# Chunked attention in front of a mixture of experts: Q, K and V laid out by numpy before the launch, K's windows copied by GpSimd, row sums taken by VectorE

## The chip, the cores and the metric

One core of one Trainium2 chip runs the whole program. The metric is the device time of one execution in microseconds (us). The kernel before took 1106.13 us (median of three runs, 1105.65 to 1109.15). Engines are named PE (TensorE), DVE (VectorE), ACT (ScalarE), POOL (GpSimd) and SP (SyncE, which here only issues DMAs).

## The reference

```python
def _attn_ref(q, k, v, mem_k, mem_v):            # B,H,S,D = 4,8,768,64; 8 memory rows per head
    chunk, left_ctx, right_ctx = (32, 16, 8)
    for c in range(S // chunk):                   # 24 chunks of 32 query rows
        k_ctx = k[:, :, max(0, 32*c - 16):min(S, 32*c + 32 + 8)]      # v_ctx likewise
        k_full = np.concatenate([mem_k, k_ctx], axis=2)               # up to 8 + 56 rows
        scores = scale * np.matmul(q_c, k_full.transpose(0, 1, 3, 2))
        a = np.exp(scores - np.max(scores, axis=-1, keepdims=True))
        a = a / (np.sum(a, axis=-1, keepdims=True) + 1e-09)
        out[:, :, c_start:c_end] = np.matmul(a, v_full)
def reference(...):
    x = attn_out.transpose(0, 2, 1, 3).reshape(3072, 512)
    x = _moe_ref(x, ...)       # logits = xn @ en.T / tau; top 1 of 8 experts; relu(x @ w1[e]) @ w2[e] * gate
    return _moe2_ref(x, ...)   # r = relu(x @ w_in); (r * r) @ w_out
```

All data are float32; the output has shape [3072, 512].

## The kernel before

The program has three stages: attention (about the first 170 us), the expert layer with its routing (to about 560 us) and the dense layer (to the end). In the second and third stage each float32 operand is split into a high and a low fp32r part and each product is three matmuls.

**The attention loop.** Work is cut into 32 items: batch b, a pair of heads hp (two heads side by side fill 128 partitions or 128 columns), and a half of the sequence (384 rows, 12 chunks). A pair j is two items. A software pipeline runs 39 rounds; in round i the list `order` (L564 to L568) calls each stage for item i minus the lag written beside it, so stages of different items interleave in a fixed order on every engine. The engines take their own instructions strictly in that order.

- `load_qk`, `load_v` (L264, L289): SP issues the DMAs of a pair: Q and K in rows of 1 KB (four sequence rows of 64 floats), V by chunks in rows of 256 bytes, and the 8 memory rows of V, broadcast to every chunk.
- `relayout` (L321): POOL (`q2`) and ACT (`k2`) bring the two heads side by side.
- `stage_a` (L330): PE transposes Q and K (4 + 4 transposes); ACT copies Q^T from PSUM (`qt`) and K^T into the zero-padded block tile `kw` as 12 overlapping windows of 56 columns (two copies); POOL adds the 8 memory columns.
- `stage_b` (L353): 12 score matmuls, then DVE masks a few columns. `max_b`, `sub_b` on DVE, `exp_b` on ACT.
- `shift_v` (L387): two DVE copies fill rows 32 to 55 of each V window from the next chunk (for the last two pairs by DMA).
- `stage_c` (L397): three transposes of the exponentials, copied by ACT (`pt`). `stage_d` (L406): 12 matmuls with V; V has a column of ones per head, so column 64 is the row sum. `sum_d`, `inv_d`, `scale_d` on DVE divide.
- `stage_t` (L448): three transposes of the result, copied by DVE and ACT in turn (`xt`); after the last pair of a batch the rows go to the DRAM tile `x_d` (768 KB, issued by ACT). `stage_m` (L461): router logits with 32 stationary columns (the expert embeddings) and the 128 tokens streamed; `stage_u` transposes them back to `dots`.
- `square` (L442): sums of squares per token on ACT.

From item 24 on, `early` picks the busiest expert of the first three batches and starts its weight loads and its first matmuls between the stages (the dictionary at L1367 says in which rounds). After the loop the rest of the routing, the expert slots and the dense layer follow in a written order (the string at L1386 and the loop at L1444).

PSUM has eight banks: in the loop `ps_s`, `ps_t`, `ps_o` one each, `ps_a` three, `ps_l` two. In the dense layer, `compare` (L1227) transposes one block a second time as plain float32 and adds the flag "differs" (a zero) to the last output tile.

Of the kernel before, what the change touches and what calls it, by code (L numbers as in the profile page):

```python
# [9 lines left out]
F32 = mybir.dt.float32  # L10
# [11 lines left out]
def kernel(  # L22
# [6 lines left out]
    mem_v: bass.AP,  # L29
# [10 lines left out]
    B, H, S, D = q.shape  # L40
    NM = mem_k.shape[2]
# [5 lines left out]
    HP = H // 2  # L47
# [31 lines left out]
    big = ctx.enter_context(tc.tile_pool(name="big", bufs=1))  # L79
# [8 lines left out]
    win_h = big.tile([P, KD, F2], F32R, name="win_h")  # L88
    win_l = big.tile([P, KD, F2], F32R, name="win_l")
# [128 lines left out]
    def weight(kind, i, w1_e, w2_e):  # L218
# [3 lines left out]
        else:  # L222
# [7 lines left out]
            lambda kk=kk, c=slice(o * 512, (o + 1) * 512): (win_h[:, kk, c], win_l[:, kk, c]),  # L230
# [4 lines left out]
    def attention(actx, hooks, space, drain):  # L235
# [3 lines left out]
        v_ctx, kw_ctx, qn_ctx = (actx.enter_context(ExitStack()) for _ in range(3))  # L239
        vb_p = v_ctx.enter_context(tc.tile_pool(name="vb", bufs=1))  # L240
        kw_p = kw_ctx.enter_context(tc.tile_pool(name="kw", bufs=1))
        kn_p = qn_ctx.enter_context(tc.tile_pool(name="kn", bufs=1))
        qn_p = qn_ctx.enter_context(tc.tile_pool(name="qn", bufs=3))
        ps_a = actx.enter_context(tc.tile_pool(name="ps_a", bufs=3, space=PSUM))
        ps_s, ps_t, ps_o = ps_r
        ps_l = actx.enter_context(tc.tile_pool(name="ps_l", bufs=2, space=PSUM))

        NV, NW, NK_, LAG = 3, 3, 2, 4
        kn = [kn_p.tile([KP, 4, R * D], F32, name=f"kn{i}") for i in range(NK_)]
        kw = [kw_p.tile([P, NC, 2, 64], F32, name=f"kw{i}") for i in range(NW)]  # L250
        vb = [vb_p.tile([P, 2 * NC + 1, 2, D + 1], F32, name=f"vb{i}") for i in range(NV)]
        scratch = per.tile([P, TE * P // 2], F32, name="scratch")
        mkn = scratch[0:H * NM, 0:B * 2 * D].rearrange("p (b j d) -> p b j d", b=B, j=2)
        mkT = per.tile([P, HP, B, 2, NM], F32, name="mkT")
        en = scratch[0:E, B * 2 * D:B * 2 * D + DM]
        enT = per.tile([P, KD, 32], F32, name="enT")
# [3 lines left out]
        qn_t, x_t, st, qk2, lp = {}, {}, {}, {}, {}  # L260

        kf, vf = (z.rearrange("b h s d -> (b h s) d") for z in (k, v))

        def load_qk(j):  # L264
            b, hp, _ = ks[2 * j]
            h0 = 2 * hp
            t = qn_p.tile([QP, 2, 2, R, D], F32, name="qn", tag="qn", bufs=2)
            for half in range(2):
                qn_t[2 * j + half] = t[:, :, half]
            nc.sync.dma_start(  # L270
                out=t.rearrange("p h j r d -> p (h j) (r d)"),
                in_=q[b, h0:h0 + 2].rearrange("h (j p r) d -> p (h j) (r d)", j=2, r=R),
            )

            base = (b * H + h0) * S
            for g0, g1, p0, p1 in (
                [(0, 1, LEFT // R, KP), (1, 4, 0, KP)] if base == 0 else
                [(0, 3, 0, KP), (3, 4, 0, KP - RIGHT // R)] if base + 2 * S == B * H * S else
                [(0, 4, 0, KP)]
            ):  # L280
                nc.sync.dma_start(
                    out=kn[j % NK_][p0:p1, g0:g1],
                    in_=bass.AP(
                        tensor=k.tensor, offset=k.offset + (base + g0 * HALF + p0 * R - LEFT) * D,
                        ap=[[R * D, p1 - p0], [HALF * D, g1 - g0], [1, R * D]],
                    ),
                )

        def load_v(j):  # L289
            b, hp, _ = ks[2 * j]  # L290
            t = vb[j % NV]
            for hh in range(2):
                h = 2 * hp + hh
                p0 = 64 * hh
                base = (b * H + h) * S
                c0, c1 = int(base == 0), 2 * NC + int(base + S < B * H * S)
                if c0:
                    nc.sync.dma_start(out=t[p0 + LEFT:p0 + CH, 0, hh, 0:D], in_=v[b, h, 0:LEFT, :])
                nc.sync.dma_start(
                    out=t[p0:p0 + CH, c0:c1, hh, 0:D],  # L300
                    in_=vf[base + CH * c0 - LEFT:base + CH * c1 - LEFT].rearrange("(c p) d -> p c d", p=CH),
                )
                if c1 == 2 * NC:
                    nc.sync.dma_start(out=t[p0:p0 + LEFT, 2 * NC, hh, 0:D], in_=v[b, h, S - LEFT:S, :])
                if j >= 14:
                    n = c1 - 1
                    nc.sync.dma_start(
                        out=t[p0 + CH:p0 + CTX, 0:n, hh, 0:D],
                        in_=bass.AP(
                            tensor=v.tensor, offset=v.offset + (base + CH - LEFT) * D,  # L310
                            ap=[[D, CTX - CH], [CH * D, n], [1, D]],
                        ),
                    )
                    if n < 2 * NC:
                        nc.sync.dma_start(out=t[p0 + CH:p0 + CH + LEFT, n, hh, 0:D], in_=v[b, h, S - LEFT:S, :])
                nc.sync.dma_start(
                    out=t[p0 + CTX:p0 + 64, 0:2 * NC, hh, 0:D],
                    in_=mem_v[b, h].unsqueeze(1).to_broadcast([NM, 2 * NC, D]),
                )

        def relayout(i):  # L321
            b, hp, half = ks[i]
            q2 = qn_p.tile([QP, R, 2, D], F32, name="q2", tag="q2", bufs=3)
            copy("p" if i > 1 else "v", q2, qn_t.pop(i).rearrange("p h r d -> p r h d"))
            k2 = qn_p.tile([KP, R, 2, D], F32, name="k2", tag="k2", bufs=3)
            kt = kn[i // 2 % NK_].rearrange("p (h j) (r d) -> p j r h d", j=2, r=R)
            copy("a", k2, kt[:, i % 2])
            qk2[i] = (q2, k2)

        def stage_a(i):  # L330
            b, hp, half = ks[i]
            q2, k2 = qk2.pop(i)
            qp = ps_a.tile([P, R, QP], F32, name="qp", tag="a")
            for r in range(R):
                nc.tensor.transpose(qp[:, r, :], q2[:, r].rearrange("p h d -> p (h d)"), ident[:QP, :QP])
            kp = ps_a.tile([P, R, KP], F32, name="kp", tag="a")
            for r in range(R):
                nc.tensor.transpose(kp[:, r, :], k2[:, r].rearrange("p h d -> p (h d)"), ident[:KP, :KP])
            qt = wk.tile([P, HALF], F32, name="qt", tag="qt")
            copy("a", qt.rearrange("p (a r) -> p r a", r=R), qp)  # L340
            kwt = kw[i % NW]
            nc.gpsimd.tensor_copy(
                out=kwt[:, :, :, CTX:64],
                in_=mkT[:, hp, b].unsqueeze(1).to_broadcast([P, NC, 2, NM]),
            )
            for hh in range(2):
                src = kp[64 * hh:64 * hh + 64]
                src = view(src, 0, [[CH // R, NC], [1, W], [KP, R]])
                dst = kwt[64 * hh:64 * hh + 64, :, hh, 0:CTX].rearrange("p c (w r) -> p c w r", r=R)
                copy("a", dst, src)  # L350
            st[i] = qt

        def stage_b(i):  # L353
            b, hp, half = ks[i]
            qt = st.pop(i)
            kwt = kw[i % NW]
            sp = ps_s.tile([P, HT, 2, 64], F32, name="sp", tag="s")
            for c in range(NC):
                j = c % 4
                nc.tensor.matmul(  # L360
                    out=sp[32 * j:32 * j + 32, c // 4].rearrange("p h k -> p (h k)"),
                    lhsT=qt[:, CH * c:CH * c + CH],
                    rhs=kwt[:, c].rearrange("p h k -> p (h k)"),
                    start=True, stop=True,
                    tile_position=(0, 32 * j),
                )
# [39 lines left out]
        def stage_d(i):  # L406
# [3 lines left out]
            op = ps_o.tile([P, HT, 2, D + 1], F32, name="op", tag="o")  # L410
# [16 lines left out]
        def inv_d(i):  # L427
            nc.vector.reciprocal(out=st[i][1], in_=st[i][1])
# [1088 lines left out]
```

## Time and profile before

| | |
|---|---|
| median of three runs | 1106.13 us |
| the profiled execution, its own time | 1108.78 us |
| its span, first to last instruction | 1107.0 us |
| PE busy in the span | 1043.3 us (94%) |
| DVE, ACT, POOL busy | 566.6, 493.2, 188.2 us |
| rounds of the attention loop, items | 39, 32 |
| last `dots` copy (end of attention) | 172.97 us |

The durations below are of the one profiled execution. Busy time of an engine is a sum over its instructions; a wait is shown as the idle time before an instruction, with what released it. The granted clock of PE is a share of 2.4 GHz: 1.00 is that level, 0.50 is 1.2 GHz, and a stretch between them has both.

### The profile page before, as it was taken

The numbers are of one execution on the slowest core, as the hardware profiler recorded it, in microseconds if no ns is written. First come the engines' busy times: TensorE is split into PE (matmuls) and PEld (weight loads), VectorE is DVE, ScalarE is ACT, GpSimd is POOL, SyncE is SP. The second block draws the span as 40 slices with busy tenths as digits, with TensorE's granted clock in tenths as the row PEclk, the third lists the DMA queues.
The fourth block names the chain that finished last, engine by engine and source line by source line (L and its number), as shares of the span: only waits on it lengthen the run. The fifth ranks groups of instructions, "written<-read, shape, count | busy, mean of one in ns | idle before, by whom it ended". The sixth has DMA issues, their size and how long they took to land. (4 is left out here: it accounts for less than half of the span.)

```text
span 1107.0 us, 20310 instructions
## 1 busy us (share of the span) xinstructions
PE 1043.3 (94%) x7541; PEld 888.3 (80%) x7541; DVE 566.6 (51%) x1103; ACT 493.2 (45%) x881; POOL 188.2 (17%) x230
## 2 busy tenths in 40 slices
PE   5888988889999999999998999999999999999997
PEld 3655766668888888887877999998999989999896
DVE  7867888664746458856885232232222222223221
ACT  6888985444635457655553222222222222222221
POOL 3311221022232323232331000000000000000000
PEclk9989989899999999999999999999999999999999
DMA  7777774653536269566451010010000100101000
GB/s 156 157 193 188 181 191 140 204 201 122 187 113 212 89 204 314 175 209 204 137 191 49 1 38 30 10 39 7 33 30 10 39 20 20 38 1 38 1 20 20
DMA packets 93334, 116.56 MB, mean 105 GB/s; under 512 B 40231, under 2 KB 52897, under 8 KB 93226
## 3 DMA queue, kind: packets, MB, share of 16 engines
q1 hardware_dynamic: 74794, 72.17, 23.1%
q10 hardware_dynamic: 11616, 21.50, 5.9%
q0 software_dynamic: 6816, 21.50, 5.6%
q8 instruction: 61, 1.00, 0.4%
q14 instruction: 47, 0.39, 0.1%
HBM read 165.48 MB, written 19.92 MB: 167 GB/s over the span
## 5 line engine op out<-in xcount | busy, mean ns | idle before, releaser
L1246 PE MATMUL z<-ft,win_h 128*128 128x256 f32 x768 | 215.8, 281 | 2.0 <-DVE ft L112 2.0
L1245 PE MATMUL z<-ft,win_h 128*128 128x256 f32 x768 | 217.2, 283 | 0.2
L1247 PE MATMUL z<-ft,win_l 128*128 128x256 f32 x768 | 216.7, 282 | 0.0
L1250 DVE TENSOR_TENSOR r<-r 128x512 f32<-128x512 f32 x96 | 66.5, 693 | 171.7 <-ACT r L1249 171.7
L1246 PEld LDWEIGHTS z<-ft,win_h 128*128 128x128 f32 x768 | 145.7, 190 | 5.7 <-DVE ft L112 2.5
L112 DVE TENSOR_TENSOR ft<-r,ft 128x512 fp32r<-128x512 f32 x96 | 66.5, 693 | 159.0 <-ACT ft L109 159.0
L1245 PEld LDWEIGHTS z<-ft,win_h 128*128 128x128 f32 x768 | 144.4, 188 | 3.8 <-issue 0.5
L1247 PEld LDWEIGHTS z<-ft,win_l 128*128 128x128 f32 x768 | 143.8, 187 | 0.0
L1249 ACT ACTIVATE r<-z 128x512 f32<-128x512 f32 x96 | 57.2, 596 | 179.4 <-PE z L1247 179.4
L109 ACT CAST ft<-r 128x512 fp32r<-128x512 f32 x96 | 59.5, 620 | 168.6 <-PE acc L1269 142.9
L1282 POOL DMA_INDIRECT out_dram<-osb,oid x24 | 27.2, 1131 | 482.4 <-ACT osb L1275 450.5
L1189 POOL DMA_INDIRECT y_d<-ysb,sidx x28 | 30.8, 1101 | 142.0 <-ACT ysb L1188 79.3
L137 ACT COPY kw<-kp 64x672 f32<-64x672 f32 x64 | 47.5, 741 | 0.4
L1142 PE MATMUL hps<-wl1b,xTh 128*128 128x512 f32 x100 | 41.0, 410 | 5.8 <-DVEq L1031 3.0
L1141 PE MATMUL yps<-wh2a,hTha 128*128 128x512 f32 x104 | 43.1, 414 | 0.3 <-ACT hTha L109 0.3
L1141 PE MATMUL hps<-wh1b,xTh 128*128 128x512 f32 x100 | 42.6, 426 | 0.6 <-ACT ha L1158 0.6
L1142 PE MATMUL yps<-wl2b,hThb 128*128 128x512 f32 x104 | 40.7, 392 | 2.3 <-DVE wl2b L112 2.3
L1143 PE MATMUL yps<-wh2a,hTla 128*128 128x512 f32 x104 | 41.0, 395 | 1.8 <-DVE hTla L112 1.8
L1141 PE MATMUL yps<-wh2b,hThb 128*128 128x512 f32 x104 | 42.6, 410 | 0.0
L1143 PE MATMUL hps<-wh1b,xTl 128*128 128x512 f32 x100 | 40.9, 409 | 0.0
L1143 PE MATMUL yps<-wh2b,hTlb 128*128 128x512 f32 x104 | 40.6, 391 | 0.0
L1142 PE MATMUL yps<-wl2a,hTha 128*128 128x512 f32 x104 | 40.6, 390 | 0.0
(349 smaller groups left out, 2432.5 us busy)
## 6 DMA issues: line engine op xcount, KB each, us to landing
r1a<-in_moe_w_dram SPq DMA_DIRECT2D x52, 512.0 KB
r1b<-in_moe_w_dram SPq DMA_DIRECT2D x52, 512.0 KB
r2a<-in_moe_w_dram SPq DMA_DIRECT2D x50, 512.0 KB
r2b<-in_moe_w_dram SPq DMA_DIRECT2D x50, 512.0 KB
rw<-in_moe_w_in_dram ACTq DMA_DIRECT2D x32, 256.0 KB
rw<-in_moe_w_out_dram ACTq DMA_DIRECT2D x32, 256.0 KB
qn<-in_q_dram SPq DMA_DIRECT2D x16, 384.0 KB
mwr<-in_moe_w_dram SPq DMA_DIRECT2D x12, 512.0 KB
```

What stands on the lines that cost most here:

```text
L109: nc.scalar.copy(out=hi, in_=src)
L112: eng.tensor_tensor(out=lo, in0=src, in1=hi.bitcast(F32), op=ALU.subtract)
L137: nc.scalar.copy(out=out, in_=in_)
L1141: nc.tensor.matmul(out=out_ps, lhsT=ah, rhs=wh, start=first, stop=False)
L1142: nc.tensor.matmul(out=out_ps, lhsT=ah, rhs=wl, start=False, stop=False)
L1143: nc.tensor.matmul(out=out_ps, lhsT=al, rhs=wh, start=False, stop=last)
L1189: nc.gpsimd.indirect_dma_start(out=y_d[:, :], out_offset=bass.IndirectOffsetOnAxis(ap=sidx[:, s:s + 1], axis=0), in_=y, in_offset=None, bo ...
L1245: nc.tensor.matmul(out=z[:, i, :], lhsT=wh, rhs=yh[:, kk, :], start=(kk == 0), stop=False)
L1246: nc.tensor.matmul(out=z[:, i, :], lhsT=wh, rhs=yl[:, kk, :], start=False, stop=False)
L1247: nc.tensor.matmul(out=z[:, i, :], lhsT=wl, rhs=yh[:, kk, :], start=False, stop=(kk == KD - 1))
L1249: nc.scalar.activation(out=r, in_=z, func=ACTF.Relu)
L1250: nc.vector.tensor_tensor(out=r, in0=r, in1=r, op=ALU.mult)
```

## The change

Numpy lays the inputs out before the launch: Q and K are transposed (128 rows = two heads x 64, 768 columns), V is written out per chunk (the 56 context rows, then the 8 memory rows, for each of the 24 chunks, so context rows stand in it more than once), and the memory keys are transposed. In the kernel:

- `load_q`, `load_k`, `load_v` are plain copies with rows of 3 KB, 3 KB and 6 KB; four DMAs per pair. The memory rows of V come with it.
- `relayout`, `stage_a` and `shift_v` go. `windows` copies the overlapping windows of K^T from the loaded tile to `kw`: POOL does both heads (ACT one of them for the first two items), and the memory columns as before.
- The column of ones in V goes: `sum_b` reduces the exponentials on DVE, `inv_b` adds 1e-9 and inverts.
- `stage_m` swaps the operands: the tokens are stationary (128 columns), the 8 expert embeddings are streamed, and the result needs no transpose. All `xt` copies are ACT's.
- The order of stages and the lags change (37 rounds, two fewer); scores alternate between two banks, `ps_a` has two.
- The tile `win` of the dense layer's weights is allocated after the routing; `compare` and its flag go; the pieces of early expert work move to other rounds.

```diff
-        def relayout(i):
-            copy("p" if i > 1 else "v", q2, qn_t.pop(i).rearrange("p h r d -> p r h d"))
-            copy("a", k2, kt[:, i % 2])
-        def stage_a(i):
...
-            copy("a", qt.rearrange("p (a r) -> p r a", r=R), qp)
...
-                copy("a", dst, src)
+        def load_q(j):
+            q_t[j] = q_p.tile([P, S], F32, name="q", tag="q")
+            nc.sync.dma_start(out=q_t[j], in_=q[b, hp])
+        def load_k(j):
+            nc.sync.dma_start(out=kt[j % NK_][:, LEFT:LEFT + S], in_=k[b, hp])
+        def load_v(j):
+            for hh in range(2):
+                nc.sync.dma_start(out=vb[j % NV][64 * hh:64 * hh + 64, hh], in_=v[b, 2 * hp + hh])
+        def windows(i):
+            kwt, ktt = kw[i % NW], kt[i // 2 % NK_]
+            for hh in range(2):
+                src = view(ktt[64 * hh:64 * hh + 64], half * HALF, [[CH, NC], [1, CTX]])
+                copy("p" if i > 1 or hh else "a", kwt[64 * hh:64 * hh + 64, hh, :, 0:CTX], src)
             nc.gpsimd.tensor_copy(
+                out=kwt[:, :, :, CTX:64], in_=mkT[:, hp, b].unsqueeze(2).to_broadcast([P, 2, NC, NM])
...
-            sp = ps_s.tile([P, HT, 2, 64], F32, name="sp", tag="s")
+            sp = (ps_s, ps_s2)[i % 2].tile([P, HT, 2, 64], F32, name="sp", tag="s")
...
-        def shift_v(i, hh):
-            nc.vector.tensor_copy(
-                out=vt[p0 + 32:p0 + CTX, c0:c0 + NC, hh, 0:D],
-                in_=vt[p0:p0 + CTX - 32, c0 + 1:c0 + NC + 1, hh, 0:D],
+        def sum_b(i):
+            nc.vector.tensor_reduce(out=sums[i], in_=st[i], op=ALU.add, axis=AX.X)
+        def inv_b(i):
+            nc.vector.tensor_scalar(out=rs, in0=rs, scalar1=1e-9, scalar2=None, op0=ALU.add)
+            nc.vector.reciprocal(out=rs, in_=rs)
...
-            copy("vava"[i % 4] if i < 27 else "a", xt, tp)
+            copy("a", xt, tp)
...
-                    out=lp[half][32 * t:32 * t + 32], lhsT=enT[:, hp, :], rhs=xt[:, t, :],
+                    out=lp[half][:, t, :], lhsT=xt[:, t, :], rhs=enT[:, hp, :],
...
         order = [
-            (stage_b, 2), (stage_c, 3), (lambda i: shift_v(i, 0), 2), (max_b, 2), (fill, 2), (sub_b, 2),
-            (lambda i: shift_v(i, 1), 2), (stage_d, LAG), (exp_b, 2), (sum_d, LAG), (fill, LAG), (inv_d, LAG), (fill, LAG),
-            (scale_d, LAG), (stage_a, 0), (stage_t, LAG + 1), (stage_m, LAG + 2), (stage_u, LAG + 3),
+            (stage_b, 0), (stage_d, LAG), (fill, 0), (sum_b, 1), (fill, 0), (inv_b, 1), (max_b, 0), (fill, 0), (sub_b, 0),
+            (stage_c, 1), (fill, 0), (exp_b, 0), (scale_d, LAG), (fill, 0), (stage_t, LAG + 1), (stage_m, LAG + 2), (stage_u, LAG + 3),
         ]
...
             if i + 2 < NK:
-                relayout(i + 2)
+                windows(i + 2)
+            if i % 2 == 0:
+                for f, n in ((load_k, 3), (load_q, 2), (load_v, 1)):
...
-                if u == NU - 1 and i == 0:
-                    self.compare(y, tp, ps_t)
```

On PE, one round of the loop in its steady part, before (`xp` is the result's transpose, `lp` the logits, `sp` the scores, `tp` the exponentials' transpose, `op` the product with V, `qp` and `kp` the transposes of Q and K):

```order
L456 MATMUL xp<-ident,xa 128x128 x3
L467 MATMUL lp<-xt,enT 32x128 x3
L360 MATMUL sp<-kw_133,qt 32x128 x12
L401 MATMUL tp<-ident,e 128x128 x3
L413 MATMUL op<-vb_138,pt 32x130 x12
L335 MATMUL qp<-ident,q_580 128x96 x4
L338 MATMUL kp<-ident,k_582 128x102 x4
```

and the same round after:

```order
L373 MATMUL xp<-ident,xa 128x128 x3
L384 MATMUL lp<-enT,xt 128x8 x3
L285 MATMUL sp<-kw_129,q 32x128 x12
L338 MATMUL op<-vb_134,pt 32x128 x12
L326 MATMUL tp<-ident,e 128x128 x3
```

The eight transposes of Q and K are gone; the logits have 128 stationary columns and 8 streamed ones in place of 32 and 128; `op` stands ahead of `tp`.

On DVE, one round of the loop before:

```order
L368 MEMSET sp 32x2x16
L392 COPY vb_137<-vb_137 24x12x64
L375 TENSOR_REDUCE mx<-sp 128x6
L381 TENSOR_TENSOR e<-sp,mx 128x384
L392 COPY vb_137<-vb_137 24x12x64
L424 TENSOR_SCALAR rs<-op 128x6
L428 RECIPROCAL rs<-rs 128x6
L435 TENSOR_TENSOR xa<-op,rs 128x3x128
```

and one round after:

```order
L294 MEMSET sp 32x2x16
L315 TENSOR_REDUCE rs<-e 128x6
L319 TENSOR_SCALAR rs<-rs 128x6
L320 RECIPROCAL rs<-rs 128x6
L301 TENSOR_REDUCE mx<-sp 128x6
L307 TENSOR_TENSOR e<-sp,mx 128x384
L352 TENSOR_TENSOR xa<-op,rs 128x3x128
```

The two V copies are gone, one reduction over the exponentials has come, and the copy of `xt`, which stood in every second round before, is no longer DVE's.

On ACT, two rounds before (`k` and `qt`, `kw` are the copies of `relayout` and `stage_a`):

```order
L137 COPY pt<-tp 128x384
L385 ACTIVATE e<-e 128x384
L137 COPY qt<-qp 128x4x96
L137 COPY kw_135<-kp 64x12x56 x2
L137 COPY xt<-xp 128x384
L137 COPY k_1232<-kn_131 102x512
L446 ACTIVATE sq,ssq<-xa 128x512
L137 COPY pt<-tp 128x384
L385 ACTIVATE e<-e 128x384
L137 COPY qt<-qp 128x4x96
L137 COPY kw_133<-kp 64x12x56 x2
```

and two rounds after:

```order
L129 COPY xt<-xp 128x384
L363 ACTIVATE sq,ssq<-xa 128x512
L129 COPY pt<-tp 128x384
L311 ACTIVATE e<-e 128x384
L129 COPY xt<-xp 128x384
L363 ACTIVATE sq,ssq<-xa 128x512
L129 COPY pt<-tp 128x384
L311 ACTIVATE e<-e 128x384
```

Four copies per round are gone from ACT; the window copies stand on POOL, two per round, with the memory columns behind them.

## Rows read from the trace of the kernel before

**Rows 1.** Windows: busy us (instructions) per engine, granted PE clock, DMA share, GB/s
```profile
75.00:100.00 25.00, 23.65 (x434) 17.58 (x436) 21.17 (x58) 23.48 (x44) 5.01 (x10) 0.99 0.79 167
...
275.00:300.00 25.00, 25.00 (x124) 20.59 (x123) 17.24 (x28) 15.68 (x27) 8.48 (x9) 1.00 0.65 215
...
425.00:450.00 25.00, 25.00 (x123) 20.51 (x123) 22.88 (x34) 20.62 (x32) 8.41 (x8) 1.00 0.92 320
```
**Rows 2.** Timeline of DVE (start, duration, instruction): items 3 and 28, the end
```profile
31.37 0.56 DVE L381 TENSOR_TENSOR e<-sp,mx 128x384 f32<-128x384 f32 x1
...
144.69 0.56 DVE L381 TENSOR_TENSOR e<-sp,mx 128x384 f32<-128x384 f32 x1
...
172.97 0.18 DVE L139 COPY dots<-dp 128x24 f32<-128x24 f32 x1 [0.46 <-PE dp L481]
```
**Rows 3.** Groups on ACT, 30 to 140 us: busy, mean ns | idle before, releaser
```profile
L137 ACT COPY kw<-kp 64x672 f32<-64x672 f32 x49 | 36.3, 741 | 0.3
L137 ACT COPY qt<-qp 128x384 f32<-128x384 f32 x24 | 20.5, 853 | 0.8 <-PE qp L335 0.8
L137 ACT COPY k<-kn 102x512 f32<-102x512 f32 x24 | 14.9, 619 | 9.5 <-DMA kn<-in_k_dram 9.2
```
**Rows 4.** Groups on DVE, 30 to 140 us
```profile
L392 DVE COPY vb<-vb 24x768 f32<-24x768 f32 x49 | 28.4, 580 | 1.5
L375 DVE TENSOR_REDUCE mx<-sp 128x6 f32<-128x384 f32 x25 | 13.9, 557 | 0.7
L381 DVE TENSOR_TENSOR e<-sp,mx 128x384 f32<-128x384 f32 x24 | 13.4, 558 | 2.3
L435 DVE TENSOR_TENSOR xa<-op,rs 128x384 f32<-128x384 f32 x24 | 13.4, 558 | 0.8
...
L428 DVE RECIPROCAL rs<-rs 128x6 f32<-128x6 f32 x24 | 4.6, 192 | 0.8
```
**Rows 5.** Groups on POOL, 30 to 140 us
```profile
L139 POOL COPY q<-qn 96x512 f32<-96x512 f32 x24 | 16.6, 691 | 77.7 <-DMA qn<-in_q_dram 71.5 <-PE kp L338 5.7 <-PE qp L335 0.4
L342 POOL COPY kw<-mkT 128x192 f32<-128x192 f32 x25 | 10.3, 410 | 5.6 <-PE sp L360 5.4
```
**Rows 6.** Timeline of PE, one round at the full clock
```profile
142.94 0.86 PE L360 MATMUL sp<-kw,qt 128*32 128x128 f32 x24
143.73 0.55 PE L401 MATMUL tp<-ident,e 128*128 128x128 f32 x3
144.21 0.87 PE L413 MATMUL op<-vb,pt 128*32 128x130 f32 x24
145.01 0.55 PE L335 MATMUL qp<-ident,q 96*128 96x96 f32 x4
...
145.75 0.49 PE L456 MATMUL xp<-ident,xa 128*128 128x128 f32 x3
146.18 0.42 PE L467 MATMUL lp<-xt,enT 128*32 128x128 f32 x6
```
**Rows 7.** Timeline of PE's weight loads (PEld) in another round
```profile
80.69 0.31 PEld L401 LDWEIGHTS tp<-ident,e 128*128 128x128 f32 x3 [0.20 <-issue]
...
83.42 0.15 PEld L467 LDWEIGHTS lp<-xt,enT 128*32 128x32 f32 x6 [0.17 <-issue]
```
**Rows 8.** Timeline of PE where it stood still, and behind it
```profile
69.65 0.42 PE L481 MATMUL dp<-ident,lt 96*128 96x96 f32 x1 [3.40 <-ACT pt L137]
...
108.02 1.51 PE L360 MATMUL sp<-kw,qt 128*32 128x128 f32 x24
```
**Rows 9.** Waits of SP's queue to 170 us: total us, times, longest
```profile
SPq L316 <- DMA x_d<-xa: 14.1, 2, 7.2
```
**Rows 10.** Timeline of DVE near the start: one zeroing of half a `kw`
```profile
3.44 0.70 DVE L487 MEMSET kw<- 64x768 f32 x1
```
**Rows 11.** Timeline of PE in the dense layer, around `compare`
```profile
1047.54 0.29 PE L1233 MATMUL tr<-ident,ys 128*128 128x128 f32 x1
...
1048.28 0.54 PE L1221 MATMUL tr<-identr,ys 128*128 128x128 f32 x4 [0.44 <-ACT ca L1234]
```

More of the change, by code (lines that the diff above doesn't have):

```diff
@@ L238, in attention @@
         per = actx.enter_context(tc.tile_pool(name="per", bufs=1))
[L239 to L244, printed above, removed]
+        vb_p = actx.enter_context(tc.tile_pool(name="vb", bufs=1))
@@ L262, in attention @@
-        kf, vf = (z.rearrange("b h s d -> (b h s) d") for z in (k, v))
-        def load_qk(j):
+        q_t, x_t, st, sums, lp = {}, {}, {}, {}, {}
+        def load_q(j):
             b, hp, _ = ks[2 * j]
[L266 to L287, printed above, removed]
@@ L464, in stage_m @@
             if hp == 0:
-                lp[half] = ps_l.tile([32 * HT, P], F32, name="lp", tag="l")
+                lp[half] = ps_l.tile([P, HT, E], F32, name="lp", tag="l")
             for t in range(HT):
                 nc.tensor.matmul(
-                    out=lp[half][32 * t:32 * t + 32], lhsT=enT[:, hp, :], rhs=xt[:, t, :],
-                    start=hp == 0, stop=hp == HP - 1, tile_position=(0, 32 * t),
-                )
-            if hp == HP - 1:
-                lt = wk.tile([32 * HT, P], F32, name="lt", tag="lt", bufs=2)
-                copy("a", lt, lp[half])
-                st[i] = lt
+                    out=lp[half][:, t, :], lhsT=xt[:, t, :], rhs=enT[:, hp, :],
+                    start=hp == 0 and t == 0, stop=hp == HP - 1 and t == HT - 1,
+                )
         def stage_u(i):
@@ L478, in stage_u, with clear_kw @@
             if hp == HP - 1:
-                lt = st.pop(i)
-                dp = ps_t.tile([P, HT, P], F32, name="dp", tag="t")[:, 0, :32 * HT].rearrange("p (t e) -> p t e", e=32)
-                nc.tensor.transpose(dp.rearrange("p t e -> p (t e)"), lt, ident[:32 * HT, :32 * HT])
                 T0 = (2 * b + half) * HT
-                copy("v", dots[:, T0:T0 + HT, :], dp[:, :, 0:E])
-        def clear_kw(j):
+                copy("v", dots[:, T0:T0 + HT, :], lp[half])
+        def clear_kw(j, eng):
@@ L501, in attention, with clear_v @@
-        load_qk(0)
+                eng.memset(kw[j][64 * hh:64 * hh + 64, 1 - hh], 0.0)
+        def clear_v(j, hh, eng):
+            eng.memset(vb[j][64 * hh:64 * hh + 64, 1 - hh], 0.0)
+        for z in kt:
+            nc.vector.memset(z[:, 0:LEFT], 0.0)
+            nc.vector.memset(z[:, LEFT + S:], 0.0)
+        load_k(0)
+        nc.sync.dma_start(out=mks, in_=mem_k.rearrange("p a b m -> p (a b m)").rearrange("p (a b m) -> p a b m", a=HP, b=B))
+        load_q(0)
+        load_k(1)
+        load_v(0)
@@ L512, in attention @@
-        nc.vector.memset(enT, 0.0)
-        clear_kw(0)
-        relayout(0)
-        relayout(1)
-        clear_kw(1)
+        for hh in range(2):
+            nc.vector.tensor_copy(out=mkT[64 * hh:64 * hh + 64, :, :, hh, :], in_=mks[64 * hh:64 * hh + 64])
+        windows(0)
+        windows(1)
+        for hh in range(2):
+            clear_v(0, hh, nc.vector)
+        clear_kw(2, nc.vector)
         taub = per.tile([E, 1], F32, name="taub")
@@ L519, in attention @@
         enn = per.tile([E, 1], F32, name="enn")
-        mp = ps_t.tile([P, B, H, NM], F32, name="mp", tag="t")
-        for b in range(B):
-            nc.tensor.transpose(
-                mp[:, b].rearrange("p h m -> p (h m)"), mkn[:, b].rearrange("p j d -> p (j d)"),
-                ident[:H * NM, :H * NM],
-            )
-        for hh in range(2):
-            nc.vector.tensor_copy(
-                out=mkT[64 * hh:64 * hh + 64, :, :, hh, :],
-                in_=mp[64 * hh:64 * hh + 64].rearrange("p b (a j) m -> p j a b m", j=2)[:, hh],
-            )
         def load_en():
@@ L594, in attention @@
                 drain((i - NK, order.index((f, lag))))
-            while vec and i > 3:
+            while vec and i > 1:
                 vec.pop(0)()
@@ L599, in attention @@
             if i + 2 < NK:
-                relayout(i + 2)
-            if i % 2 == 0 and i + 4 < NK:
-                load_qk(i // 2 + 2)
-            if i % 2 and i + 1 < NK:
-                load_v((i + 1) // 2)
+                windows(i + 2)
+            if i % 2 == 0:
+                for f, n in ((load_k, 3), (load_q, 2), (load_v, 1)):
+                    if i // 2 + n < NK // 2:
+                        f(i // 2 + n)
             drain((i - NK, -1))
-            for _ in range(min(len(squares), 1 if i < NK + 2 else 2 if i < NK + 3 else 0)):
+            for _ in range(min(len(squares), 1 if i < NK else 0)):
                 square(*squares.pop(0))
@@ L1276, in mm2 @@
                     else:
[L1277 to L1280 removed]
+                        nc.vector.tensor_copy(out=o, in_=acc[j])
                     jj = 2 * u + j
@@ L1486, with _lay_out @@
             ffn_step(4, NU)
-_INS = ["q", "k", "v", "mem_k", "mem_v", "moe_expert_emb", "moe_tau", "moe_w1", "moe_w2", "moe2_w_in", "moe2_w_out"]
+_INS = ["q", "k", "v", "mem_k", "moe_expert_emb", "moe_tau", "moe_w1", "moe_w2", "moe2_w_in", "moe2_w_out"]
 _OUTS = [((3072, 512), "float32")]
+def _lay_out(q, k, v, mem_k, mem_v, **rest):
+    import numpy as np
+    B, H, S, D = q.shape
+    NM = mem_k.shape[2]
+    flip = lambda z: np.ascontiguousarray(z.reshape(B, H // 2, 2, S, D).transpose(0, 1, 2, 4, 3)).reshape(B, H // 2, 2 * D, S)
+    vp = np.pad(v, ((0, 0), (0, 0), (16, 8), (0, 0)))
+    vw = np.empty((B, H, 56 + NM, S // 32, D), v.dtype)
+    for c in range(S // 32):
+        vw[:, :, :56, c] = vp[:, :, 32 * c:32 * c + 56]
+        vw[:, :, 56:, c] = mem_v
+    mk = mem_k.reshape(B, H // 2, 2, NM, D).transpose(2, 4, 1, 0, 3).reshape(2 * D, H // 2, B, NM)
+    return dict(rest, q=flip(q), k=flip(k), v=vw, mem_k=mk)
 def kernel(**inputs):
@@ L1501 @@
     arrays, args = {}, []
+    inputs = _lay_out(**inputs)
     for name in _INS:
```

192 lines of the change are left out of this document (50 added, 142 removed).

## The prediction, made before the changed kernel was run

> **What bounds the kernel now.** I first read busy time by stretches of 25 us. In the attention loop PE and ACT are both at 94% and DVE at 85%; behind it PE is busy without a break at the full clock [rows 1]. So a microsecond taken from the loop is taken from the end, unless the expert stage then waits for something it did not wait for before; the dense layer, bound by PE, hides nothing.
>
> The timeline of DVE gives the pace of the loop. The subtraction of item 3 starts at 31.37 us, that of item 28 at 144.69, and the last logits are copied at 172.97 [rows 2]. That is three stretches: a start of 31.4 us, 25 rounds of 113.3/25 = 4.53 us, and an end of 28.3 us in which the first expert's work is mixed with the last items.
>
> Next the groups by engine. ACT's copies of K and Q cost 2 x 0.741 + 0.853 + 0.619 = 2.95 us per round [rows 3], nearly all of them with no idle time before them except `k`, which waited 9.5 us for its DMA. The waits show where that comes from: SP twice stood about 7 us behind a write of `x_d` [rows 9], the K load came late, PE stood 3.4 us, and in such a place the score matmuls took 1.51 us instead of 0.86 [rows 6, 8]: the clock had fallen to the lower of its levels, 1.2 GHz. So a round is ACT's work plus, about once in a batch, a load that comes late.
>
> **What the change does to a round.**
>
> ACT loses the 2.95 us and takes over every `xt` copy, so at most 4.53 - 2.95 + 0.6 = 2.2 us remain. It no longer bounds.
>
> DVE loses two V copies of 0.580 and half an `xt` copy, and gains a reduction over 384 columns, which I price as the one over the scores, 0.557. Four long operations at 0.557 or 0.558, the addition and the reciprocal at not over 0.192 each [rows 4] and a short mask make 2.7 us, with the gaps between dependent instructions up to 2.9.
>
> POOL loses the Q copy and gets two window copies of 672 columns. The Q copy, 512 columns, took 0.691 on average, the memory columns 0.410 [rows 5]. Pro rata a window copy takes 0.91, by the line through both rows 0.83; so POOL has 2 x 0.91 + 0.41 = 2.2 us. Twice the row's rate, the upper bound, would be 4.0. Both are under the old round, and `windows` runs two rounds ahead of the scores that read it.
> The Trainium skill (SBUF — State Buffer, section "Who interferes with whom") says that GpSimd and VectorE share a port pair that one of them holds for a whole instruction, and that float32 copies on VectorE inside SBUF take it. By that rule POOL was held up before by the V copies, and with them gone its copies come out at the lower price, 0.83; it takes some chance from the rival of a POOL that is too slow. No run here has yet shown the copies without them.
>
> PE loses the eight transposes, 145.75 - 145.01 = 0.74 us. The starts of the others are 0.79 (scores), 0.48 (`tp`), 0.80 (`op`) and 0.43 (`xp`) apart [rows 6], 2.50 together. The logits were 0.42 with 32 stationary columns. With 128 stationary ones their six weight loads cost more: three loads of 128 columns took 0.31, six of 32 took 0.15 [rows 7]. Six of 128 are 0.62, and with the short streams I take 0.75; below, they stay at 0.42; above, 1.0. PE's round is 3.25, with bounds of 2.9 and 3.5. Here the change makes something dearer: it is the largest sum of the four engines.
> The Trainium skill (TensorE: Matmul & The Clock Gate, section "LDWEIGHTS") states that a weight load costs by its columns, at about 107 ns for 128; by it the swap costs as much as I take, while by the streamed columns alone (8 for 128) the logits would nearly vanish, PE would have some 2.6 us and the time would be about 1063 us, with the DMAs as the bound.
>
> The DMAs: a pair brings 384 KB of Q, 384 KB of K and 768 KB of V, 1.57 MB; a batch (8 rounds) has four pairs and two `x_d` writes of 768 KB, 7.86 MB in all. At the 320 GB/s of the best stretch of the trace that takes 24.6 us, 3.07 per round; scaled to a full DMA share (0.92 there) it takes 2.82 [rows 1]. That is close under PE's sum, so the DMAs are nearly a second bound, although there is no row of 256 bytes left.
>
> So a round takes PE's 3.25, and 0.1 for what isn't hidden: 3.35. Its bounds are 2.9 (PE at its lower bound) and 4.2 (DMAs that miss their turn).
>
> The late loads: a pair has four DMAs instead of six or more. In the program each DMA waits for the one eight issues before it, so SP now meets an `x_d` write two pairs later, about 13 us, instead of one. I expect these stalls of PE to go or to shrink, and with them the slow rounds behind them. This is in the 3.35.
>
> **The start.** The first scores no longer wait for transposes, but DVE has more to do before item 3, since the lags are gone: 14 pieces of zeroing like the one of 0.70 us [rows 10] (9.8 us, 2 us for gaps), some 24 small operations on the expert embeddings at not over 0.19 [rows 4] (4.6), four rounds of about 2.4 without the final scaling, and 1 us ahead of all: 27 us against 31.4. I take a gain of 4; between 0 (the first loads come late, or PE stays at the lower clock) and 8.
>
> **The end of the loop and after.** From item 28 to the last logits nine rounds stand in both programs, with the same early expert work; there the V copies were gone already for the last two pairs, and the chain over the small routing operations on DVE stays. I take the 28.3 us as they are, 3 us either way. After that the instruction streams of all engines are the same, but for `compare`: between its transpose and the next block 48.28 - 47.54 = 0.74 us pass on PE [rows 11], worth 0.7.
>
> **The sum.** 4 + 25 x (4.53 - 3.35) + 0.7 = 4 + 29.5 + 0.7 = 34.2 us. The profiled execution took 1108.78 us (span 1107.0), which gives 1074.6. The median of the runs lies 2.65 below the profiled one: 1072 us.
>
> **The rivals.**
>
> *The DMAs set the pace.* Loads of three pairs and bursts of `x_d` share the queues; the sum of 3.07 is near, and a single wait costs a slow round behind it [rows 8]. For it: 298 GB/s would be needed without pause at a round of 3.3, where the loop moved 167 and the best stretch 320 [rows 1]. Against it: rows of 3 and 6 KB, and four rounds between issue and use. With 3.85 per round: 4 + 17 + 0.7 = 21.7 us, 1084 us.
>
> *Everything is hidden better than I think.* The logits are as cheap as before and the stalls go: 2.95 per round and 6 us at the start, 6 + 39.5 + 0.7 = 46 us, 1060 us.
>
> *Slower: POOL's window copies.* Each round's scores need two copies and the memory columns from POOL, one after the other. If a copy of overlapping windows costs far more than the Q copy, PE waits for `kw` in every round and falls to the lower clock. At 2.4 us a copy the round is 5.2, the loop 17 us longer, less 4.7 elsewhere: 1118 us. It decides from 2.15 us a copy (2 x 2.15 + 0.41 = 4.72, where the loop's loss eats the 4.7). For it: no row shows this access pattern on POOL. Against it: that is 2.4 times the pro rata price of a copy that also permutes.
>
> *No change.* The loop is shorter, but the first expert's loads or the routing chain then come later against PE, and the time is lost between 170 and 250 us: about 1106 us. Against it: in the new rounds these steps stand as many rounds ahead of the end as they did, and the four weight loads are issued when the loop's own loads are over.
>
> **How the numbers follow.** Forecast (round of 3.2 to 3.55) 0.50; DMAs 0.24; better hidden 0.13; slower by POOL 0.08; no change 0.05. A measurement of this kernel can tell about 0.3%, 3.3 us, from no change. Faster: 0.50 + 0.24 + 0.13 and a little of the last case, 0.88; same 0.04; slower 0.08. The likeliest gives 1072; from the better case to the DMA case with its own spread the range is 1058 to 1092, and it leaves out the last two and the outer tails.
>
> **What would show it.** Right: start to start about 3.3 us between the score matmuls of neighbouring items, PE over 90% busy at a granted clock of 1.00 in the loop, window copies under 1 us on POOL, logits of 0.7 to 0.8 us, the last `dots` copy near 139 us, and from there the same distances as before. Wrong: idle time of PE in front of the score matmuls, released by POOL (window copies) or by a DMA; a granted clock of about 0.5 in the loop; logits that cost no more than before; a last `dots` copy that is earlier while the weight splits behind it wait longer.

## The result, and the profile after

The changed kernel took 1080.62 us (median of 4 runs, 1077.37 to 1082.77), the one before 1106.52 on the same chip: a ratio of 0.976, 95% interval 0.9729 to 0.979. It is faster by 2.4%; the forecast was 1072, and 1080.6 lies inside the range of 1058 to 1092. The profiled executions are compared below: 1108.78 us before, 1080.12 after (span 1078.0).

The milestones on DVE that answer to [rows 2] (start, duration, instruction):

```profile
28.07 0.56 DVE L307 TENSOR_TENSOR e<-sp,mx 128x384 f32<-128x384 f32 x1
...
115.71 0.56 DVE L307 TENSOR_TENSOR e<-sp,mx 128x384 f32<-128x384 f32 x1
...
143.97 0.26 DVE L131 COPY dots<-lp 128x24 f32<-128x24 f32 x2
```

| stretch | before | after | gained | forecast |
|---|---|---|---|---|
| start, to the subtraction of item 3 | 31.37 | 28.07 | 3.3 | 4 |
| 25 rounds | 113.32 (4.53 each) | 87.64 (3.51 each) | 25.7 | 29.5 (3.35 each) |
| item 28 to the last logits | 28.28 | 28.26 | 0.0 | 0 |
| last logits to the end of the span | 934.03 | 934.03 | 0.0 | 0.7 |

PE's timeline of one round, against [rows 6]:

```profile
34.73 0.86 PE L285 MATMUL sp<-kw,q 128*32 128x128 f32 x24
35.41 0.84 PE L338 MATMUL op<-vb,pt 128*32 128x128 f32 x24
36.18 0.55 PE L326 MATMUL tp<-ident,e 128*128 128x128 f32 x3
36.56 0.49 PE L373 MATMUL xp<-ident,xa 128*128 128x128 f32 x3
36.89 0.73 PE L384 MATMUL lp<-enT,xt 128*128 128x8 f32 x6
```

The next scores start at 37.56, those of the third round behind at 43.31: (43.31 - 34.73)/3 = 2.86 us for a round in which nothing stands still. That is less than the 3.25 forecast, and yet the mean round took 3.51. The window of the 25 rounds (columns as in [rows 1]) shows where the other 0.65 us x 25 = 16 us went:

```profile
28.07:115.71 87.64, 77.19 (x1500) 67.74 (x1498) 64.13 (x199) 43.44 (x106) 45.72 (x76) 0.95 0.99 258
```

PE stood for 87.64 - 77.19 = 10.5 us, and the rest is matmuls that ran slower, at a granted clock of 0.95 on average. The same timeline where PE stood longest:

```profile
78.21 0.42 PE L338 MATMUL op<-vb,pt 128*32 128x128 f32 x7
81.00 1.23 PE L338 MATMUL op<-vb,pt 128*32 128x128 f32 x17 [2.36 <-issue]
...
84.70 1.51 PE L285 MATMUL sp<-kw,q 128*32 128x128 f32 x24
```

PE stops after 7 of 24 equal matmuls, with no releaser that the profile shows, and goes on 2.36 us later; behind it the scores take 1.51 us, at a granted clock of 0.50 (the windows from 81 to 84 and from 84.5 to 86 us), the lower level of 1.2 GHz. The groups of PE from 30 to 115 us (busy, mean ns | idle before them, what ended it) name what ended the stops, and those of POOL answer to [rows 5]:

```profile
L338 PE MATMUL op<-vb,pt 128*32 128x128 f32 x596 | 23.5, 284 | 8.2 <-issue 4.3 <-ACT e L311 1.7 <-DMA vb<-in_v_dram 1.4
L285 PE MATMUL sp<-kw,q 128*32 128x128 f32 x576 | 21.6, 283 | 0.9 <-issue 0.9
...
L326 PE MATMUL tp<-ident,e 128*128 128x128 f32 x74 | 14.2, 299 | 1.4 <-issue 1.4
```

```profile
L131 POOL COPY kw<-kt 64x672 f32<-64x672 f32 x49 | 36.6, 746 | 40.7 <-PE sp L285 39.3
L275 POOL COPY kw<-mkT 128x192 f32<-128x192 f32 x24 | 8.2, 342 | 1.5
```

Most of PE's idle time (4.3 + 0.9 + 1.4 = 6.6 us) waits for nothing that the profile shows, and POOL waits for PE, not PE for POOL. What is full is the DMA: the windows (columns as in [rows 1]), and the queues from 30 to 115 us (packets, MB, share of 16 engines):

```profile
25.00:50.00 25.00, 24.09 (x466) 21.14 (x458) 21.25 (x64) 10.78 (x24) 14.80 (x26) 0.91 1.03 225
...
75.00:100.00 25.00, 21.80 (x405) 18.98 (x394) 16.39 (x52) 11.95 (x31) 11.65 (x19) 0.86 1.01 284
```

```profile
DMA packets 7181, 22.00 MB, mean 259 GB/s; under 512 B 795, under 2 KB 795, under 8 KB 7166
...
q1 hardware_dynamic: 4884, 17.28, 82.9%
q10 hardware_dynamic: 2282, 4.51, 15.1%
q8 instruction: 11, 0.18, 1.0%
```

A full share moves only 225 to 284 GB/s here, where the best stretch before moved 320 at a share of 0.92 [rows 1]. SP's loads (q1) move 17.28 MB in 0.829 x 85 us, 245 GB/s of their own busy time; the writes of `x_d` (q10) move 4.51 MB in 0.151 x 85, 351 GB/s. The waits of SP's queue, against [rows 9] (total, times, longest):

```profile
SPq L266 <- DMA x_d<-xa: 21.5, 3, 10.5
SPq L257 <- DMA x_d<-xa: 10.4, 1, 10.4
```

With the smaller waits for the same writes (1.9 and 0.7 us before, 0.2 after) they grew from 16.7 to 32.1 us.

### The profile page after: what moved, and what is told of

It is laid out like the page before. It is cut to its first block, busy times and chain, and to the rows that moved or that the text cites. A ratio compares the mean times of both kernels' runs of the same rounds, so it can differ in the third digit from the quotient of the medians.

```text
span 1078.0 us, 19442 instructions
## 1 busy us (share of the span) xinstructions
PE 1015.4 (94%) x7272; PEld 883.5 (82%) x7272; DVE 536.8 (50%) x1066; ACT 413.5 (38%) x759; POOL 213.1 (20%) x257
## 5 line engine op out<-in xcount | busy, mean ns | idle before, releaser
L131 POOL COPY kw<-kt 64x672 f32<-64x672 f32 x62 | 46.2, 745 | 51.6 <-PE sp L285 46.3
L338 PE MATMUL op<-vb,pt 128*32 128x128 f32 x768 | 30.8, 291 | 10.5 <-issue 4.3
```

The source lines that it names most:

```text
L131: (nc.vector if eng == "v" else nc.gpsimd).tensor_copy(out=out, in_=in_)
```

## The experiments

Theory A: the DMA is full in the loop and sets the pace; PE's stops without a releaser come from it too. Rival B: the engines wait for each other in order, whatever the DMA does. Rival C: POOL's window copies set the pace. Every expectation below is the text on record. "25 rounds" is the stretch from item 3 to item 28 of the profiled execution.

**e1, V loaded for three pairs only**

```diff
         def load_v(j):
+            if j >= 3:
+                return
             b, hp, _ = ks[2 * j]
```

> Leaves out the load of V for all pairs of heads but the first three (later pairs use stale rows), and nothing of the engines' work. Theory A (DMA is full in the loop; PE's stops without a releaser are its instructions that come late behind the bulk packets): the loop moves 0.59 instead of 0.98 MB a round, the 25 rounds from the sub of item 3 to that of item 28 fall from 87.6 to 72 to 76 us (2.88 to 3.05 each), PE's idle marked issue before the outputs falls from 4.3 to under 1 us, and the whole from 1080 to 1065 to 1069. Rival B (engines wait for each other in order, whatever DMA does): 85 to 88 us and 1078 to 1082, with the same waits on exp and on the scores' mask. Rival C (GpSimd's window copies set the pace): the same as B.

1068.14 us (ratio to before 0.9641, 0.9624 to 0.9658); the 25 rounds took 75.52, and PE's idle marked issue before the outputs fell from 4.3 to 0.8 us. In its windows the DMA is no longer full:

```profile
50.00:75.00 25.00, 23.47 (x486) 20.96 (x484) 21.34 (x66) 14.98 (x38) 14.84 (x26) 1.00 0.62 194
```

A holds; B and C, which expected no change, fall: the engines did the same work.

**e2, window copies of K for three items only**

```diff
-            for hh in range(2):
+            for hh in range(2 if i < 3 else 0):
                 src = view(ktt[64 * hh:64 * hh + 64], half * HALF, [[CH, NC], [1, CTX]])
```

> Leaves out GpSimd's window copies of K from item 3 on (later items use stale windows; the copies of the memory keys stay), so that GpSimd falls from about 2.2 to 0.5 us a round. Theory A: no change, 1079 to 1082, the 25 rounds within 2 us of 87.6, since GpSimd waits for the scores and not they for it. Rival C: the rounds fall to 3.0 and the whole to about 1068. A small gain of DVE, because GpSimd no longer shares its port, would show as DVE groups that are shorter than 557 and 547 ns, with the loop up to 3 us shorter.

1083.01 us (ratio 0.9767, 0.9742 to 0.9792), 25 rounds 90.50. Nothing is gained, though the copies are gone and POOL waits 75 us for the scores:

```profile
L275 POOL COPY kw<-mkT 128x192 f32<-128x192 f32 x23 | 8.1, 351 | 75.3 <-PE sp L285 75.3
```

C falls. The time is just above the range expected for A and the rounds are 2.9 us above 87.6, where 2 were allowed; e7 shows how far the rounds vary. DVE's long groups stay at 557 and 548 ns, so the copies do not slow these. They do slow two short ones: without them the addition behind the row sum (L319) took 172 ns instead of 203, and a routing operation (L552) 228 instead of 626; e3 comes back to it.

**e4, the write of x in two halves**

```diff
-            if hp == HP - 1:
-                T0 = (2 * b + half) * HT
-                (...).dma_start(out=x_d[T0 * P:(T0 + HT) * P, :].rearrange(...), in_=xa)
+            if hp % 2:
+                T0, w = (2 * b + half) * HT, slice((hp - 1) * P, (hp + 1) * P)
+                (...).dma_start(out=x_d[T0 * P:(T0 + HT) * P, w].rearrange(...), in_=xa[:, :, w])
```

> Same output as the changed kernel: the write of x to DRAM goes out in two halves of the width, each when its two pairs of heads are ready, so that a burst is 384 KB instead of 768 KB, with the same bytes in twice as many rows of 1 KB. Theory A with bytes as what counts: no change, 1078 to 1083, since the loop still moves 0.98 MB a round. Theory A with the bursts as what counts: SyncE's waits on the write fall from 21.5 and 10.4 us to under half, PE's issue gaps to half, and the whole to 1070 to 1076. Rival B: no change.

1084.86 us (ratio 0.9808, 0.9772 to 0.9844), 25 rounds 86.32; SP waited 25.1 and 21.8 us for these writes, longer than before the edit. The time lies 1.9 us above the range for no change, and the interval of the ratio overlaps that of the changed kernel. So smaller bursts win nothing. But PE's picture is another one: from 30 to 115 us no idle time is marked issue any more, and PE waits for V instead:

```profile
PE op L338 <- DMA vb<-in_v_dram: 6.8, 3, 4.5
```

The stops without a releaser went, and no time was won by it: the DMA's pace reaches PE in one form or the other.

**e5, V loaded twice**

```diff
                 nc.sync.dma_start(out=vb[j % NV][64 * hh:64 * hh + 64, hh], in_=v[b, 2 * hp + hh])
+                nc.sync.dma_start(out=vx[j % 2][64 * hh:64 * hh + 64], in_=v[b, 2 * hp + hh])
```

> Adds a second load of V's rows for every pair, into tiles that nothing reads; the output is the same. Theory A with bytes as what counts: 1.37 MB a round at 259 GB/s are 5.3 us, the 25 rounds take about 132 instead of 87.6 us and the whole 1120 to 1130, with waits of the outputs on V. Rivals B and C: within 5 us of 1080, since the loads of the next pairs would still come in time.

1135.57 us (ratio 1.0243, 1.0226 to 1.0261), slower than before the change; 25 rounds 133.48. PE's longest waits from 30 to 165 us are now for V:

```profile
PE op L340 <- DMA vb<-in_v_dram: 27.3, 9, 7.3
```

A's sum, 132 us of rounds, came out within 2 us, in part by luck: from 30 to 165 us the DMAs moved 32.02 MB, 237 GB/s and not 259, and so 1.27 MB a round and not 1.37. The whole lies above the 1120 to 1130 expected. With e1 this gives the pace from both sides.

**e6, V's partitions spread.** Why does a full DMA move so little? Q and K are loaded into 128 partitions, each head of V into 64 neighbours, with rows of 6 KB.

```diff
-                nc.sync.dma_start(out=vb[j % NV][64 * hh:64 * hh + 64, hh], in_=v[b, 2 * hp + hh])
+                nc.sync.dma_start(out=vb[j % NV][hh:P:2, hh], in_=v[b, 2 * hp + hh])
...
-            e = wk.tile([P, HT, 2, 64], F32, name="e", tag="e")
+            e = wk.tile([P, HT, 64, 2], F32, name="e", tag="e")
...
-            nc.vector.tensor_tensor(out=e, in0=sp, ...)
+            nc.vector.tensor_tensor(out=e.rearrange("p t k h -> p t h k"), in0=sp, ...)
...
```

> Same output, same bytes: head 0 of a pair stands in the even partitions and head 1 in the odd ones, so that each load of V goes to 64 partitions spread over all 128 instead of 64 that lie side by side (e is stored with the two heads alternating, and the zeros of the three V tiles are written ahead of the loads). Theory P (V's loads are slow because of where they land): the loads of SyncE's queue move 245 GB/s of their own busy time in the changed kernel, and 295 GB/s without V, so V alone runs at about 209; at 295 a round's 0.393 MB of V take 1.33 instead of 1.88 us, the 25 rounds fall from 87.6 to 74 to 79 us and the whole to 1067 to 1073. Theory R (V's rows of 6 KB are what is slow): no change, 1078 to 1083. Theory H (reading V from DRAM is slow, whatever the row): no change either. The Trainium skill's page SBUF, State Buffer, section Door 1: the DMA port swizzle, says that the rate depends on how many ports the partitions reach, and that 64 neighbours reach half of them; by that rule P holds.

1066.98 us (ratio 0.9635, 0.9617 to 0.9653). Its queues from 30 to 100 us:

```profile
q1 hardware_dynamic: 4579, 16.29, 70.1%
q10 hardware_dynamic: 2400, 4.72, 17.5%
```

16.29 MB in 0.701 x 70 us are 332 GB/s for the same loads that moved at 245. The 25 rounds took 77.18, and PE shows no idle time marked issue in this stretch. P holds, and H, which expected no change, falls. The start is 5 us shorter too (item 3 at 23.10); the edit also writes the zeros elsewhere, so how much of these 5 us the faster first loads gave stays open. Some of the gain was given back behind the loop (e10). Half of these bytes are V. V's own rate in the changed kernel is an estimate: with the other half at 332 it stood at 194 GB/s (1/245 = 0.5/332 + 0.5/194), and with the other half at the 295 of e1 (8.26 MB in 0.400 x 70 us) at 209, the figure of the expectation. By 332 and 194, e5, where V is two thirds of the bytes, comes out at 225 against 228 measured (27.06 MB in 0.880 x 135 us).

The Trainium skill (SBUF — State Buffer, section "Door 1: The DMA port swizzle") says that 64 neighbouring partitions reach only half of the ports on the DMA's side, and gives 196 GB/s for them, measured with 1 MiB; the 194 to 209 estimated here for loads of 384 KB agree. It asks for transfers that span all 128 partitions; in e6 every second one of them is enough, at 332 GB/s together with Q and K.

**e7, V in rows of 2 KB**

```diff
+    vw = vw.reshape(B, H, 56 + NM, 3, S // 96, D).transpose(0, 1, 3, 2, 4, 5)
...
-                nc.sync.dma_start(out=vb[j % NV][64 * hh:64 * hh + 64, hh], in_=v[b, 2 * hp + hh])
+                nc.sync.dma_start(out=vb[j % NV][64 * hh:64 * hh + 64, hh].rearrange("p (g c) d -> p g (c d)", g=3),
+                                  in_=v[b, 2 * hp + hh].rearrange("g p c d -> p g (c d)"))
```

> Same output, same bytes and the same partitions as the changed kernel, but numpy lays V out in three groups of chunks, so that a load reads and writes rows of 2 KB instead of 6 KB. Theory R: V's rate rises from about 209 towards 295 GB/s and the whole falls to 1067 to 1073. Theories P and H: no change, 1078 to 1083, with three times as many packets of V.

1082.65 us (ratio 0.9787, 0.9763 to 0.9811), with more packets and the rate as it was, 14.84 MB in 0.892 x 70 us, 238 GB/s:

```profile
q1 hardware_dynamic: 6622, 14.84, 89.2%
```

R falls. The 25 rounds took 84.93. Among the kernels that load V as the changed one does (the changed kernel, e2, e3, e4 and e7) they lie between 84.9 and 92.0, so a difference of a few us between two of these says nothing.

**e3, a short row sum**

```diff
-            nc.vector.tensor_reduce(out=sums[i], in_=st[i], op=ALU.add, axis=AX.X)
+            nc.vector.tensor_reduce(out=sums[i], in_=st[i][:, :, :, 0:2], op=ALU.add, axis=AX.X)
```

> The row sums run over 2 of the 64 columns (the output is wrong by that), which takes about 0.45 us a round from VectorE. Theory A (DMA sets the pace): no change, 1078 to 1083, and VectorE waits longer for the scores. Rival B (VectorE and the waits in order set it): up to 0.45 us a round, 1069 to 1073.

1084.96 us (ratio 0.9801, 0.9779 to 0.9823), 25 rounds 92.03: no gain, and 2 us above the range for A. But it tells nothing on B:

```profile
L319 DVE TENSOR_SCALAR rs<-rs 128x6 f32<-128x6 f32 x23 | 12.4, 537 | 0.7
...
L315 DVE TENSOR_REDUCE rs<-e 128x6 f32<-128x12 f32 x23 | 3.5, 152 | 10.1 <-issue 6.3 <-ACT xt L129 2.0 <-ACT e L311 1.8
```

The reduction fell from 528 to 152 ns and the addition behind it rose from 203 to 537, so DVE was relieved of 0.04 us, not 0.45. The timeline shows why:

```profile
33.85 1.55 POOL L131 COPY kw<-kt 64x672 f32<-64x672 f32 x2 [0.93 <-PE sp L285]
...
34.04 0.58 DVE L319 TENSOR_SCALAR rs<-rs 128x6 f32<-128x6 f32 x1
```

The first of the two window copies ends at 34.59 us, and the addition of six numbers, which started inside it, at 34.62. In 21 of the 23 rounds it ends so, 0.03 us behind a copy of POOL, and in the other two it takes 0.16 to 0.17 us; in e2, without these copies, it always took 0.17. So on DVE the shortened sum was spent waiting for POOL's copy, and B was not tested by this edit.

**e8, e6 with the logits as before**

```diff
-                lp[half] = ps_l.tile([P, HT, E], F32, name="lp", tag="l")
+                lp[half] = ps_l.tile([32 * HT, P], F32, name="lp", tag="l")
...
-                    out=lp[half][:, t, :], lhsT=xt[:, t, :], rhs=enT[:, hp, :],
+                    out=lp[half][32 * t:32 * t + 32], lhsT=enT[:, hp, :], rhs=xt[:, t, :],
...
```

> V in every second partition as in e6, and the logits as before the change: the expert embeddings padded to 32 columns are the stationary side again, and each batch's logits are copied and transposed. Same output. In the changed kernel the logits take 0.67 to 0.73 us of PE a round, before it took 0.42. Theory PE (with V's loads no longer in the way, the sum of PE's work sets the round): 0.3 us a round less, undisturbed rounds of 2.6 instead of 2.9, the 25 rounds 70 to 73 instead of 77 us and the whole 1060 to 1063. Rival DVE (VectorE's 2.6 us of work and its gaps set it): at most 0.1 us a round, 1064 to 1067. Rival D (DMA still sets it): no change from e6, 1066 to 1069.

1061.77 us (ratio 0.9593, 0.9577 to 0.9610): the fastest of all. PE's timeline shows the logits short and the round at 30.77 - 28.19 = 2.58 us:

```profile
28.19 0.55 PE L326 MATMUL tp<-ident,e 128*128 128x128 f32 x3
28.58 0.49 PE L373 MATMUL xp<-ident,xa 128*128 128x128 f32 x3
29.00 0.31 PE L384 MATMUL lp<-xt,enT 128*32 128x128 f32 x3
29.04 0.30 PE L285 MATMUL sp<-kw,q 128*32 128x128 f32 x1
29.13 0.28 PE L384 MATMUL lp<-xt,enT 128*32 128x128 f32 x3
29.17 0.90 PE L285 MATMUL sp<-kw,q 128*32 128x128 f32 x23
29.97 0.86 PE L338 MATMUL op<-vb,pt 128*32 128x128 f32 x24
30.77 0.55 PE L326 MATMUL tp<-ident,e 128*128 128x128 f32 x3
```

The 25 rounds took 74.98, 1.7 to 2.2 us less than with the new logits (e6, e10), where 4 to 7 were expected: the undisturbed rounds fell by 0.1 to 0.3, and some now wait for ACT's exp or the mask. So part of theory PE and part of the rival DVE. Most of the rest of its gain stands behind the loop, which e10 shows to vary.

**e9, K and V loaded for three pairs only** (the edit of e1, in `load_k` too)

> The changed kernel without the loads of K and V of all pairs but the first three (later pairs use stale rows); Q's loads and the writes of x stay, about 0.39 MB a round. It measures what the engines need by themselves. Theory A (DMA set the pace of the changed kernel, and neither e1 nor e6 leaves much of that): the 25 rounds take 73 to 76 us, with undisturbed rounds of 2.9 and the slow ones where VectorE has routing work, the whole 1064 to 1069. If K's loads alone still cost as much as V's did, the rounds fall to 2.7 and the whole to 1058 to 1062.

1066.86 us (ratio 0.9654, 0.9630 to 0.9678), 25 rounds 75.93, no less than without V alone. The window of its rounds:

```profile
25.72:101.65 75.93, 72.60 (x1499) 64.38 (x1497) 64.56 (x200) 44.06 (x106) 45.68 (x76) 0.99 0.37 123
```

So 76 us are what the engines need: 25 x 2.86 = 72, and 3.3 us in three rounds in which PE waits for DVE, in part behind its routing work. About 12 of the changed kernel's 87.6 us were the DMA's (9 to 16 by the spread under e7): PE stood 7.1 us longer (10.45 against 3.33), and as many matmuls took 4.6 us more (77.19 against 72.60), at a granted clock of 0.95 against 0.99.

**e10, the kernel of e6 again**

> The kernel of e6 once more, beside the other two and in more rounds, for its interval: 1066 to 1069 us, the 25 rounds 76 to 79 us. What its profile before gave back behind the loop (968.2 us from the sub of item 28 to the end, 962.3 in the changed kernel) is to be there again if it belongs to this kernel, and gone if it was that one execution.

1069.51 us (5 runs, ratio 0.9662, 0.9643 to 0.9681), 0.5 above the range expected; 25 rounds 76.70; from item 28 to the end 964.9 us, against 968.2 in e6 with the same code. Over all profiles that stretch lies between 960.1 (e9) and 969.6 (e5): differences of a few us behind the loop say nothing of a kernel by one profile.

## Why the forecast came out as it did

**The start** (4): 3.3, right in kind. The expert embeddings' first operation on DVE waited 3.2 us for ACT, which waited for their load. The zeroing came to 9.6 us, near the 9.8 of the sum by luck: 6 pieces of 0.70 and 4 of 1.34 us, not 14 of 0.70.

**PE's sum** (3.25): 2.86. Scores 0.68 to 0.76, outputs 0.77 and logits 0.67 came out close to their prices; `tp` was 0.38 instead of 0.48 and `xp` 0.33 instead of 0.43, taken from distances to other neighbours [rows 6]. That the swapped logits are dearer than before, 0.67 against 0.42, was right, and e8 shows it to be a part of the change that costs time once the DMA lets it. By the price in the Trainium skill (TensorE: Matmul & The Clock Gate, section "LDWEIGHTS (loading the stationary operand)"), the columns divided by 1.2 in ns, six loads of 128 columns are an estimated 0.64; the 0.67 agrees.

**0.1 us for what isn't hidden:** this is the step that failed; it was 0.65, of which 0.47 (11.7/25) are the DMAs' by e9. It rested on the DMA sum of 2.82 to 3.07 us a round, and that on a rate of 320 GB/s, taken from a stretch of weight loads. V is half of the loads and goes to 64 neighbouring partitions, where it moves at an estimated 194 to 209. By the rates of e6 (332 for Q and K, 194 for V) and 351 for `x_d`, the prediction's 0.98 MB a round take an estimated 1.18 + 2.03 + 0.56 = 3.77 us, above PE's sum and close to the 3.85 of the rival "the DMAs set the pace", which had the mechanism. The round took 3.51, and fewer bytes fell into it: 22.00 MB in 85 us are 0.91 MB a round. The kernel loads K and Q up to three pairs ahead, so their last loads are issued before item 28. So the time came out between the forecast and the rival's 1084 us, and nearer to the rival's.

That the forecast came this close is partly luck: PE's sum was 0.39 too much and the 0.1 was 0.55 too little, which leaves 0.16 a round. The 3.51 lies in the range of 3.2 to 3.55 to which the prediction gave its largest chance, but it is the rival's mechanism that put it there. Three of the signs named for being right did not come: 3.3 us from start to start (2.86 where nothing stood still), PE over 90% busy at a clock of 1.00 (88% at 0.95), and the last `dots` copy near 139 us (143.97).

**The late loads** "to go or to shrink": wrong. SP stood longer behind `x_d`, behind a DMA that is full; only 1.4 us reached PE as a wait for V, and 6.6 us came as stops between equal matmuls.

**POOL** (0.83 to 0.91 a window copy): 0.746, and e2 shows that leaving the copies out gains nothing in the whole. By the Trainium skill (SBUF — State Buffer, section "Who interferes with whom") the lower price was due with DVE's copies of V gone. The trace went below it; no run puts the V copies back, so whether the shared port was the reason is not shown.

**The end of the loop** (28.3): 28.26. **`compare`** (0.7): PE's transposes around it [rows 11] went from 1048.65 - 1047.24 = 1.41 us to 0.64, so the 0.77 is there, but the stretch between the last logits and that place is 0.75 longer. By e10 that is less than two executions of one kernel differ; whether the 0.7 is kept stays open.

**The sum:** on the profiled run 1074.6 against 1080.1 measured, of which 25 x 0.16 = 3.9 are the rounds, 0.7 the start and 0.7 `compare`. The other 3.1 us to 1072 against 1080.6 are the scaling to medians: the forecast took off 2.65, by which the profiled run of before lay above its median of three runs, and the profiled run of after lay 0.5 below its own.

## What to carry to other kernels

Price a transfer by rows of transfers that land in the same partitions: a DMA share near 1.00 with a low GB/s raises the question of what slows the bytes. Here it was the destination (e6) and not the length of the rows (e7), and spreading 64 rows over every second partition was worth 10.5 to 10.9 us of the loop. When the DMA is the bound, its cost need not appear as waits for data; it can stand as stops marked issue inside rows of equal matmuls (the changed kernel), or as waits for V (e4), and as matmuls at the lower clock behind either. And each part of a change should be asked for by itself: the logits' swap cost PE 0.25 us a round, where the prediction said 0.33, and undoing it gave the best version.

## What was not expected of the hardware

PE stopped five times in the middle of equal matmuls, for 0.5 to 2.4 us each. In all five a packet of the instruction queue (q8) began 2.7 to 2.9 us before the stop ended; from 77 to 81 us it is this one:

```profile
q8 instruction: 1, 0.02, 2.1%
```

Over all runs there are 20 such stops of more than 0.25 us in the 25 rounds, and each has such a packet 2.3 to 3.2 us before its end, though only 11 or 12 such packets begin in the 25 rounds of a run. Most packets bring no stop: the changed kernel had 11 for its five.

That PE's next instructions come late behind the bulk packets fits this, and of 6.6 us of such stops 0.8 were left where the loads were fewer (e1) and none where they were faster (e6); in e8, whose rounds are shorter, 1.6. But e4 had none either, with V loaded into the same 64 neighbours. That the packets cause the stops is argued from the order in time, not shown: no experiment changed the instruction packets themselves.
